# Attention and mixture of experts on one core: rank zero's token list made on its own, its row scales moved, two ranks narrower

## The chip, the cores and the metric

One NeuronCore of a Trainium2 chip runs the whole program. The metric is the device time of one execution in microseconds; of the runs made, the median counts. The names of the engines are those of the profile: PE is TensorE, DVE is VectorE, ACT is ScalarE, POOL is GpSimd, SP is SyncE, which only issues DMAs here.

## The reference

The attention comes first: 8 x 8 heads of 576 positions with 64 numbers each, a coarse attention over means of four positions and a local one over 7 neighbours, added up. Its output is the input x of a mixture of experts: 4608 tokens with 512 numbers, four groups of four experts. A token goes to the best expert of its best group.

```python
x = np.ascontiguousarray(attn_out.transpose(0, 2, 1, 3)).reshape(B * S, H * D)
g_idx = np.argmax(x @ w_group, axis=1)
...
e_idx = np.argmax(xg @ w_expert[g], axis=1)
...
h = np.maximum(xg[mask_e] @ w1[g, e], 0.0)
ye = h @ w2[g, e]
out[tok_idx] = combined[:, None] * ye      # combined: product of the two softmax weights
```

## The kernel before

The program runs in one pass over an order written out by hand (`ORDER`), then over a second list of steps (`begin`), then over the ranks (`main`). Each engine does its instructions in the order of these lists, and a wait of one of them holds all that stands behind it on that engine.

While the attention of the last batch still runs, the expert that has most of the first three quarters' tokens, up to 256, is done as the "early" one: 256 of its rows first, and what the last quarter adds as up to 128 "late" rows. `hidden f` is one block of 128 of its 1024 hidden numbers (12 products: four parts of 128 numbers, each matrix split in a high and a low part), `project f` carries a block into the output. The other 15 experts are put in order by their number of tokens ("ranks"). `ranks` makes that order on DVE (lines 813 to 820), `rank_lists` the token lists of all ranks (`choose`, lines 788 to 792, and `targets`, lines 797 to 799): `gi` holds the rows to fetch, `oi` the rows to store to.

`begin` first lets POOL fetch rank zero's rows (`gather`, `fetch`, line 925: an indirect DMA of 128 rows into `xg`, four of them, the last one for 32 rows) and SP load the first two of four quarters of its weights (`weights_in`, line 886). Then come the steps. The late rows run in four rounds: `hidden_rows` (12 products of 256 columns, line 1003, then the copy `hr` on ACT, line 1006), `turn_hidden` (two transposes, line 1011, then the copy `hrh` on ACT and the difference `hrl` on DVE, lines 965 and 966) and `project` (three products of 512 columns, line 1036). Between them stand the steps for rank zero: `scale` (ACT, line 939) multiplies the 512 numbers of the fetched rows by the token's weight, `turn_in k` (line 972) transposes the k-th 128 of them on PE, and ACT and DVE split them into `xh` and `xl` (lines 965 and 966). `weights_split` makes the high part of a quarter of the weights on ACT (line 894) and the low part on DVE (line 898). The low part frees the buffer for SP's next load. `arms` works out on DVE, in one number (`word`), which ranks need their full width; `choice` loads that number into the engines (line 1159).

In `main`, rank r multiplies its weights by CAPS[r] columns if it has more than CAPS[r] - LESS[r] tokens, and by CAPS[r] - LESS[r] columns otherwise (an If with two arms, for the ranks in SWITCHED). A rank has 96 hidden products (line 987) and 96 projecting ones (line 1038). The first hidden product of rank zero, behind the last projection of the late rows, begins `main`.

Of the kernel before, what the change touches and what calls it, by code (L numbers as in the profile page):

```python
# [34 lines left out]
NE = 16  # L35
# [7 lines left out]

QSCALE = SCALE / 16.0
CAPS = [416, 384, 368, 352, 336, 320, 312, 304, 296, 288, 280, 272, 264, 248, 240, 384]
LESS = [16 if r == 1 else 20 for r in range(16)]
SWITCHED = (0, 1, *range(3, 13))
TURNED = range(13)
SCATTER = (1, 3, 5, 8)
# [655 lines left out]
class Experts:  # L705
# [47 lines left out]
    def numbers(self):  # L753
# [7 lines left out]
        for j in range(NE):  # L761
            nc.gpsimd.memset(self.digit[:, j : j + 1], float(2**j))
            nc.gpsimd.memset(self.less[:, j : j + 1], -float(LESS[j]))

# [44 lines left out]
    def ranks(self):  # L809
# [9 lines left out]
        V.tensor_reduce(out=self.er, in_=self.big, axis=AX.X, op=ALU.add)  # L819
        V.tensor_copy(self.eri, self.er[0:1])  # L820

    def rank_lists(self):
        self.choose(0, NE - 1, self.roh[:, 0 : NE - 1], self.gi[:, 0 : NE - 1])
        self.targets(0, NE, self.oi)

    def fours(self):
# [277 lines left out]
    def begin(self, early, late, st):  # L1104

        V = self.nc.vector
        for n in ("w1", "w2"):
            for c in range(4):
                late[n, c] = early[n, c]
        self.gather(st)  # L1110
        e = self.expert(st)
        self.weights_in(st, e, 0)
        self.weights_in(st, e, 1)
        gathered = range(len(st["xg"]))
        steps = [
            (self.store, early, 0),
            (self.store, early, 1),
            (self.hidden_rows, late, 0),
            (self.weights_high, st, 0, "w1"),
            (self.hidden_rows, late, 1),  # L1120
            (self.turn_hidden, late, 0),
            (self.arms,),
            (self.hidden_rows, late, 2),
            (self.turn_hidden, late, 1),
            (self.weights_low, st, 0, "w1", V),
            (self.project, late, 0),
            (self.project, late, 1),
            *((self.scale, st, t) for t in gathered[:2]),
            (self.hidden_rows, late, 3),
            (self.turn_hidden, late, 2),  # L1130
            *((self.scale, st, t) for t in gathered[2:]),
            (self.project, late, 2),
            (self.project, late, 3),
            (self.choice,),
            (self.project, late, 4),
            (self.weights_split, st, 0, "w2", V),
            (self.weights_in, st, e, 2),
            (self.turn_in, st, 0),
            (self.turn_in, st, 1),
            (self.turn_hidden, late, 3),  # L1140
            (self.weights_split, st, 1, "w1", V),
            (self.project, late, 5),
            (self.turn_in, st, 2),
            (self.turn_in, st, 3),
            (self.fours,),
            (self.weights_split, st, 1, "w2", V),
            (self.weights_in, st, e, 3),
            (self.project, late, 6),
            (self.project, late, 7),
            (self.store, late, 0),  # L1150
        ]
        for f, *args in steps:
            f(*args)
        self.ys = [self.results(i, [P, 4 * P]) for i in range(4)]
        for y in self.ys:
            V.memset(y[:, CAPS[0] - LESS[0] : CAPS[0]], 0.0)

# [10 lines left out]
    def main(self, late, sts):  # L1168
        none = {"C": P, "xg": [], "y": []}
        sts = sts + [None]  # L1170
        with self.tc.manual_schedule():
            for r in range(NE - 2):
                pv = sts[r - 1] if r else none
                if r in SWITCHED:
# [3 lines left out]
                    with arm.Else():  # L1178
                        here[0] = dict(here[0], arm=CAPS[r] - LESS[r])
                        self.ranked(pv, *here, self.hint(r + 1))  # L1180
# [321 lines left out]
logits 15; scores_out 3; hidden 1; scores_turn 3; project 0; scores_turn_out 3; choose 3; choose_exp 3; choose_first 3; weight 3; hidden 2  # L1502
project 1; places 3; places_out 3; project 2; weights_split 2 w1 P; lists_places 3; lists 3 P; count 3; weights_split 2 w2 P; hidden 3
hidden 4; hidden 5; lists_add 3; early_list 0; gather_late; weights_split 3 w1 D; project 3; weights_split 3 w2 D; project 4; ranks
project 5; hidden 6; turn_late 0; turn_late 1; hidden 7; turn_late 2; turn_late 3; rank_lists; project 6; project 7
"""

@with_exitstack
# [111 lines left out]
```

## Time and profile before

| | us |
|---|---|
| median of 3 runs | 673.28 |
| lowest and highest | 669.38, 678.78 |
| the profiled execution | 675.54 |
| its span, first to last instruction | 673.8 |

The rows in this document are of the profiled execution. Times in a row count from the start of its span; 1.7 us of the profiled time lie outside the span. The mean granted TensorE clock was 0.988 of full speed.

### The profile page before, as it was taken

The page shows a single profiled execution, that of the slowest core. Times are in us where ns is not written, and L with a number is a line of the kernel's source. Part 1 is how long each engine was busy: PE and PEld are TensorE (multiplying, and loading weights), DVE is VectorE, ACT ScalarE, POOL GpSimd, SP SyncE. Part 2 cuts the span into 40 slices and gives each one's busy share as a digit, 9 for nine tenths or more (in the row PEclk, how much of TensorE's full clock was granted, in tenths as well). Part 3 has the DMA queues.
Part 4 walks back from the last instruction along what each step waited for, and adds up shares of the span by engine and source line. Part 5 has one row for each costly group of instructions (what it writes and reads, how often), then busy time and mean ns, then how long its engine had stood idle before and what let it go on. Part 6 is the DMA issues. An engine that isn't in the chain of part 4 may idle for free. (4 is left out here: it accounts for less than half of the span.)

```text
span 673.8 us, 17810 instructions
## 1 busy us (share of the span) xinstructions
PE 638.9 (95%) x6751; PEld 574.8 (85%) x6751; DVE 475.8 (71%) x968; ACT 382.5 (57%) x831; POOL 362.8 (54%) x418
## 2 busy tenths in 40 slices
PE   7898898998988898999999999999999999999996
PEld 3675676676766687999999999999999999999985
DVE  5886788778897586746666576766776786878751
ACT  7886665766764535644535345454464565556531
POOL 7974556576642554404463746657557556654521
PEclk7999999998998999999999999999999999999999
DMA  8799799979877816868686878879889879998920
GB/s 313 205 280 286 229 276 295 281 209 256 265 219 222 253 31 232 287 216 217 222 233 203 237 228 251 243 228 286 254 261 292 256 250 266 287 306 282 286 72 29
DMA packets 125903, 160.75 MB, mean 239 GB/s; under 512 B 23133, under 2 KB 90601, under 8 KB 125792
## 3 DMA queue, kind: packets, MB, share of 16 engines
q1 hardware_dynamic: 100032, 130.01, 63.8%
q0 software_dynamic: 8240, 20.47, 10.0%
q10 hardware_dynamic: 17520, 8.85, 4.9%
q8 instruction: 62, 1.02, 0.7%
q14 instruction: 49, 0.40, 0.2%
HBM read 129.51 MB, written 30.98 MB: 238 GB/s over the span
## 5 line engine op out<-in xcount | busy, mean ns | idle before, releaser
L1063 POOL DMA_INDIRECT out_dram<-yt,qo x135 | 153.6, 1137 | 138.5 <-DVE qo L838 109.5
L991 ACT ACTIVATE hh<-ph 128x368 fp32r<-128x368 f32 (+14 forms) x128 | 52.7, 413 | 185.7 <-PE ph L987 149.6
L987 PE MATMUL ph<-xh,w1h 128*128 128x368 f32 (+14 forms) x512 | 152.6, 299 | 0.0
L987 PE MATMUL ph<-xh,w1l 128*128 128x368 f32 (+14 forms) x512 | 152.4, 298 | 0.2 <-issue 0.2
L987 PE MATMUL ph<-xl,w1h 128*128 128x368 f32 (+14 forms) x512 | 152.4, 298 | 0.1
L1038 PE MATMUL y<-hh,w2h 128*128 128x368 f32 (+11 forms) x416 | 126.2, 303 | 0.0
L1038 PE MATMUL y<-hl,w2h 128*128 128x368 f32 (+11 forms) x416 | 125.7, 302 | 0.0
L1038 PE MATMUL y<-hh,w2l 128*128 128x368 f32 (+11 forms) x416 | 125.6, 302 | 0.0
L992 DVE SCALAR_TENSOR_TENSOR hl<-ph,hh 128x368 fp32r<-128x368 f32 (+14 forms) x128 | 58.5, 460 | 85.1 <-ACT hh L991 49.8
L987 PEld LDWEIGHTS ph<-xl,w1h 128*128 128x128 f32 x512 | 96.4, 188 | 0.8
L987 PEld LDWEIGHTS ph<-xh,w1h 128*128 128x128 f32 x512 | 96.2, 188 | 1.0 <-issue 0.2
L987 PEld LDWEIGHTS ph<-xh,w1l 128*128 128x128 f32 x512 | 96.4, 188 | 0.7 <-issue 0.6
L898 DVE TENSOR_TENSOR w2l<-raww,w2h 128x1024 fp32r<-128x1024 f32 x61 | 74.7, 1225 | 22.0 <-ACT w2h L894 14.8
L898 DVE TENSOR_TENSOR w1l<-raww,w1h 128x1024 fp32r<-128x1024 f32 x61 | 74.4, 1220 | 20.5 <-ACT w1h L894 10.7
L925 POOL DMA_INDIRECT xg<-xd,gi x47 | 55.4, 1179 | 53.9 <-ACT xh L965 23.9
L1038 PEld LDWEIGHTS y<-hl,w2h 128*128 128x128 f32 x416 | 78.3, 188 | 0.1
L1038 PEld LDWEIGHTS y<-hh,w2l 128*128 128x128 f32 x416 | 78.3, 188 | 0.0
L1038 PEld LDWEIGHTS y<-hh,w2h 128*128 128x128 f32 x416 | 78.2, 188 | 0.0
L894 ACT ACTIVATE w1h<-raww 128x1024 fp32r<-128x1024 f32 x64 | 67.4, 1054 | 2.6 <-DMA raww<-in_moe_w_dram 2.1
L894 ACT ACTIVATE w2h<-raww 128x1024 fp32r<-128x1024 f32 x64 | 67.1, 1051 | 0.8 <-DMA raww<-in_w2q_dram 0.7
L460 PE MATMUL b_x<-vw,pt 126*32 126x128 f32 x1152 | 39.0, 279 | 3.6 <-DMA vw<-odd 2.2
L460 PEld LDWEIGHTS b_x<-vw,pt 126*32 126x32 f32 x1152 | 31.0, 111 | 9.0 <-issue 6.9
(243 smaller groups left out, 1183.1 us busy)
## 6 DMA issues: line engine op xcount, KB each, us to landing
raww<-in_w2q_dram SPq DMA_DIRECT2D x52, 512.0 KB
raww<-in_w1q_dram SPq DMA_DIRECT2D x52, 512.0 KB
raww<-in_moe_w_dram SPq DMA_DIRECT2D x24, 512.0 KB
vw<-in_vw_dram SPq DMA_DIRECT2D x32, 378.0 KB
kt<-in_k_dram SPq DMA_DIRECT2D x16, 576.0 KB
qT<-in_q_dram SPq DMA_DIRECT2D x16, 576.0 KB
xd<-x ACTq DMA_DIRECT2D x15, 576.0 KB
vs<-in_vm_dram SPq DMA_DIRECT2D x16, 512.0 KB
```

Source lines behind the costliest of these rows:

```text
L460: self.nc.tensor.matmul(pt[32 * j : 32 * j + 32, t], self.of("pt", u)[:ROWS, 32 * lin : 32 * lin + 32], self.windows(u)[:ROWS, :, lin], st ...
L894: self.nc.scalar.activation(hi, self.raw[c % 2][n], AF.Copy)
L898: eng.tensor_tensor(out=lo, in0=self.raw[c % 2][n], in1=hi.bitcast(F32), op=ALU.subtract)
L925: self.nc.gpsimd.indirect_dma_start(out=xg[:w], out_offset=None, in_=self.xd[0:rows], in_offset=bass.IndirectOffsetOnAxis(ap=st["gi"][:w, ...
L987: nc.tensor.matmul(ph, a[:, k, cs], st[b][:, k, 0:C], start=(n == 0), stop=(n == 11))
L991: nc.scalar.activation(hh, ph, AF.Relu)
L992: nc.vector.scalar_tensor_tensor(out=hl, in0=ph, scalar=0.0, in1=hh.bitcast(F32), op0=ALU.max, op1=ALU.subtract)
L1038: nc.tensor.matmul(y, a[:, f % 2, cs], b, start=(f == 0 and n == 0), stop=(f == 7 and n == 2))
L1063: i = self.nc.gpsimd.indirect_dma_start(out=out, out_offset=bass.IndirectOffsetOnAxis(ap=index, axis=0), in_=y, in_offset=None, bounds_che ...
```

## The change

Three things change. `ORDER` gets a step `first_list` right behind `ranks`: it makes the list `gi` of rank zero alone; `rank_lists` makes the fourteen others, and the transposes of the late tile move behind `hidden 7`. In `begin`, the scales of rank zero's first three tiles stand between the late rows' earlier rounds; the split of the first quarter of w2 and the load of the third quarter stand ahead of the late rows' `project 3`; `project 4` moves behind `turn_hidden 3` and the split of the second quarter of w1. LESS is 28 and 24 for ranks three and four instead of 20.

```diff
-LESS = [16 if r == 1 else 20 for r in range(16)]
+LESS = [20, 16, 20, 28, 24] + 11 * [20]
...
+    def first_list(self):
+        self.choose(0, 1, self.roh[:, 0:1], self.gi[:, 0:1])
+
     def rank_lists(self):
-        self.choose(0, NE - 1, self.roh[:, 0 : NE - 1], self.gi[:, 0 : NE - 1])
+        self.choose(1, NE - 1, self.roh[:, 1 : NE - 1], self.gi[:, 1 : NE - 1])
         self.targets(0, NE, self.oi)
...
             (self.arms,),
+            (self.scale, st, 0),
             (self.hidden_rows, late, 2),
             (self.turn_hidden, late, 1),
             (self.weights_low, st, 0, "w1", V),
+            (self.scale, st, 1),
+            (self.scale, st, 2),
             (self.project, late, 0),
             (self.project, late, 1),
-            *((self.scale, st, t) for t in gathered[:2]),
             (self.hidden_rows, late, 3),
             (self.turn_hidden, late, 2),
-            *((self.scale, st, t) for t in gathered[2:]),
+            *((self.scale, st, t) for t in range(3, len(st["xg"]))),
             (self.project, late, 2),
+            (self.weights_split, st, 0, "w2", V),
+            (self.weights_in, st, e, 2),
             (self.project, late, 3),
             (self.choice,),
-            (self.project, late, 4),
-            (self.weights_split, st, 0, "w2", V),
-            (self.weights_in, st, e, 2),
             (self.turn_in, st, 0),
             (self.turn_in, st, 1),
             (self.turn_hidden, late, 3),
             (self.weights_split, st, 1, "w1", V),
+            (self.project, late, 4),
             (self.project, late, 5),
...
-project 5; hidden 6; turn_late 0; turn_late 1; hidden 7; turn_late 2; turn_late 3; rank_lists; project 6; project 7
+first_list; project 5; hidden 6; hidden 7; turn_late 0; turn_late 1; project 6; turn_late 2; turn_late 3; rank_lists; project 7
```

## Rows read from the trace of the kernel before

**Rows 1.** The page, busy time of each engine and its share of the span.

```profile
PE 638.9 (95%) x6751; PEld 574.8 (85%) x6751; DVE 475.8 (71%) x968; ACT 382.5 (57%) x831; POOL 362.8 (54%) x418
```

**Rows 2.** Waits of PE, 240 to 673 us: total us, times, longest.

```profile
PE y L1036 <- ACT hrh L965: 0.9, 1, 0.9
PE xt L972 <- DMA xg<-xd,gi: 0.7, 1, 0.7
PE xt L972 <- ACT xg L939: 0.6, 1, 0.6
PE xt L972 <- DVE xl L966: 0.5, 1, 0.5
...
```

**Rows 3.** Timeline of PE: start, us, operation, count, idle before it and its releaser.

```profile
249.29 0.44 PE L972 MATMUL xt<-idf,xg 128*128 128x128 f32 x2 [0.72 <-DMA xg<-xd,gi]
...
261.49 0.38 PE L1011 MATMUL ht<-idf,hr 128*128 128x128 f32 x2
...
264.14 0.50 PE L1036 MATMUL y<-w2h,hrh 128*128 128x512 f32 x1 [0.86 <-ACT hrh L965]
...
266.25 0.90 PE L972 MATMUL xt<-idf,xg 32*128 32x32 f32 x5 [0.59 <-ACT xg L939]
...
271.32 0.34 PE L987 MATMUL ph<-xh,w1h 128*128 128x396 f32 x1
```

**Rows 4.** Timeline of POOL: the fetches of the late tile and of rank zero.

```profile
245.09 1.77 POOL L925 DMA_INDIRECT xg<-xd,gi  x1 [0.81 <-DVE gi L792]
256.44 1.00 POOL L925 DMA_INDIRECT xg<-xd,gi  x1 [9.57 <-PE phr L1003]
...
260.35 2.07 POOL L925 DMA_INDIRECT xg<-xd,gi  x1 [0.30 <-DVE flag L1282]
```

**Rows 5.** Timeline of DVE: lists, ranks, and the differences of the late rows.

```profile
243.53 0.83 DVE L788 TENSOR_TENSOR sel<-tv,early 128x64 f32<-128x64 f32 x1
...
244.66 0.17 DVE L792 TENSOR_SCALAR gi<-rv 128x4 int32<-128x4 f32 x1
...
249.71 0.16 DVE L820 CAST eri<-er 1x16 int32<-1x16 f32 x1
...
252.39 1.88 DVE L788 TENSOR_TENSOR sel<-tv,roh 128x960 f32<-128x960 f32 x1
...
255.50 0.20 DVE L792 TENSOR_SCALAR gi<-rv 128x60 int32<-128x60 f32 x1
...
260.08 0.40 DVE L966 TENSOR_TENSOR hrl<-ht,hrh 128x256 fp32r<-128x256 f32 x1
260.41 1.20 DVE L898 TENSOR_TENSOR w1l<-raww,w1h 128x1024 fp32r<-128x1024 f32 x1
...
270.99 1.08 DVE L966 TENSOR_TENSOR xl<-xt,xh 128x416 fp32r<-128x416 f32 x2
```

**Rows 6.** Timeline of ACT: a weight copy, scales, and the third round's hr.

```profile
255.94 1.05 ACT L894 ACTIVATE w1h<-raww 128x1024 fp32r<-128x1024 f32 x1
...
262.14 1.40 ACT L939 ACTIVATE xg<-xg 128x512 f32<-128x512 f32 x2 [2.82 <-DMA xg<-xd,gi]
263.45 0.36 ACT L1006 ACTIVATE hr<-phr 128x256 f32<-128x256 f32 x1
...
265.47 0.72 ACT L939 ACTIVATE xg<-xg 32x512 f32<-32x512 f32 x1 [0.78 <-DMA xg<-xd,gi]
```

**Rows 7.** Busy time by stretch (PE, PEld, DVE, ACT, POOL), granted clock, DMA share, GB/s.

```profile
250.00:260.00 10.00, 10.00 (x70) 9.24 (x69) 7.84 (x22) 4.25 (x12) 2.95 (x3) 1.00 0.76 243
```

**Rows 8.** Line 1159, the choice's load in TensorE's sequencer: duration in ns, start.

```profile
L1159 PEldq TENSOR_LOAD <-word x1: 487/487/487, 260.5 to 260.5; - x1
```

**Rows 9.** Timeline of PE: the first products of ranks three, four and five.

```profile
372.90 0.32 PE L987 MATMUL ph<-xh,w1h 128*128 128x332 f32 x1
...
402.05 0.31 PE L987 MATMUL ph<-xh,w1h 128*128 128x316 f32 x1
...
429.89 0.30 PE L987 MATMUL ph<-xh,w1h 128*128 128x300 f32 x1
```

More of the change, by code (lines that the diff above doesn't have):

```diff
@@ L1113, in begin @@
         self.weights_in(st, e, 1)
-        gathered = range(len(st["xg"]))
         steps = [
```

## The prediction

> **What bounds the kernel now.** I read the page's busy line first: TensorE is busy 95% of the span [rows 1]. The chain of waits says nothing here: it holds only GpSimd's last store. So I asked who TensorE waited for, from 240 us to the end [rows 2]. The reader is to see that every wait of size lies before rank zero starts: 0.9 us for a copy of ScalarE, 0.7 us for a fetch, 0.6 us for a scaled tile, 0.5 us for VectorE. Behind 271.32 us, where the first product of rank zero starts, TensorE never waits for another engine again. Two things follow: what the stretch from 247 to 271 us loses is lost to the end, and a column taken from a later rank shortens the end by that column.
>
> The stretch itself I read engine by engine [rows 3 to 6]. Rank zero's list is written together with the fourteen others and is ready at 255.70 (255.50 + 0.20) [rows 5]. GpSimd's first fetch starts 0.74 us later, at 256.44 (the row names a product of TensorE, which only ended last; the fetch reads the list), and the four starts are 1.30 us apart, to 260.35 [rows 4]. ScalarE then idles 2.82 us for the first tile (262.14) and 0.78 us for the last (265.47) [rows 6], and since it works in order, the late rows' copies wait behind the scales: hr of round three comes at 263.45 though its products ended near 261.5 [rows 3, 6]. TensorE pays at 264.14 (0.86), 266.25 (0.59) and a little after [rows 2, 3].
>
> **The lists.** Three VectorE instructions go in right behind the cast of the ranks, which ends at 249.87 [rows 5]. Their cost has two bounds. The early expert's list took 1.30 us (243.53 to 244.83, 0.83 of it for the first), but there GpSimd was busy with a product of its own. Undisturbed, the list product of 960 elements takes 1.88, so 64 elements are 0.13 and a fixed part; three short instructions like the third (0.17) and the cast (0.16) make 0.65 with their starts. I take 0.65, because GpSimd is idle from 246.86 to 256.44 [rows 4]. The list is then ready at 250.5 and the first fetch starts 0.74 later, at 251.3; at 1.30 apart the others start at 252.6, 253.9 and 255.2. That the other fourteen lists are written later into the same tile shouldn't hold the fetch: at 271.32 rank zero's products read the first quarter of xl while VectorE writes the last ones until 272.07 [rows 3, 5], so a reader waits for its part of a tile alone.
>
> Who waits for the 0.65: hl of the early expert's sixth block stands behind it on VectorE, ready at 250.85 instead of 250.2. In the new order the seventh block's products (12 x 256 columns x 0.42 ns = 1.3 us, the price of a column is worked out below) stand ahead of the late tile's transposes, so TensorE no longer waits 0.72 for that tile [rows 3]: it landed by 249.3. But project six now comes sooner and waits about 0.5 for hl. Together that is 0.25 saved, or 0.4 lost at the 1.30 bound. The long list work starts some 0.7 later on VectorE and hands everything behind it (the second early store, the first hrl, the arms) on up to 0.7 later. Its cover is that hrl of round one, which ended at 260.48 [rows 5], is needed by project two only behind 261.49 [rows 3]; without that 1.0 us it would cost up to 0.7.
>
> **When the tiles land.** The first fetch was usable 5.7 us after its start (256.44 to 262.14), the fourth 5.1 (260.35 to 265.47) [rows 4, 6], with the DMA engines busy with weights. From the new starts that is 257.0 for the first and 260.3 for the last, 5.2 us earlier. ScalarE reaches scale zero at 257.7 (the weight copy ends at 256.99 [rows 6], two copies of about 0.38 follow), so it waits for nothing, and nothing of hr two, queued behind it, is held up. Scales one and two lie before round three's copy, in time that ScalarE idled away. What is late next is ScalarE's own order: round three's products end with the transposes at 261.49 [rows 3], 0.25 earlier now; then come hr three (from about 261.5, 0.36), hrh two (0.38) and the last scale (0.72), which ends near 262.9 instead of 266.19.
>
> From the end of the last scale to rank zero's first product it took 5.13 us (266.19 to 271.32): the second weight split, the transposes, projects five to seven. The split is moved ahead of project three in the program, but on ScalarE it still stands right behind the last scale and ahead of the first xh, and on VectorE ahead of the first xl, so this chain keeps its length. Project four is now inside it (three products of 512 columns, 0.65) and fills the 0.5 that TensorE waited there for VectorE [rows 2]: 5.13 + 0.2 to 5.4. Rank zero then starts at 262.9 + 5.4 = 268.3, **3.0 us earlier**. Cross-check: the four named waits are 2.7 us; the restart of the stream behind each adds some 0.2 to 0.3, and 0.5 of new waiting goes off: 2.2 to 3.4.
>
> **Other queues.** The choice's load of the arm word was taken by TensorE's sequencer at 260.5, over two microseconds ahead of its place in the stream [rows 8], and stays behind project three: nothing, or at most its 0.49 us if the sequencer is no longer ahead. On SyncE the third weight load is still released by w1l (260.41 + 1.20 [rows 5]); the fourth comes about 3 us earlier with the second split, and SyncE's own loads of the choice now queue behind it, to about 265. Only SyncE's next branch needs them, behind 268. GpSimd's fetches pass nothing. The first weight load now shares the DMA engines with the first fetch: 128 rows of 2112 bytes at the 243 GB/s of 250 to 260 us [rows 7] delay it by 1.1 us at the most; ScalarE would wait that long at 255.9 and has the later idle time to take it back: 0 to 0.5.
>
> **The narrower ranks.** A rank is 192 products (96 hidden, 96 projected). From 332 to 316 columns it shrinks from 29.15 us (372.90 to 402.05) to 27.84 us (402.05 to 429.89) [rows 9]: 1.31 / 16 = 0.082 us a column, 0.42 ns for each product. Eight columns are 0.66, four 0.33: **0.98 us**, all on the path. It holds only while both lists fit: over 324 rows rank three would run at 352, over 312 rank four at 336. Counted from the reference's own inputs and rules, these lists have 312 and 305 rows, so the narrow arms stay.
>
> **Sum.** 3.0 + 0.98 = 4.0 us off the profiled execution: 675.54 becomes 671.5. That run lay 2.26 above the median of the three, 673.28, which becomes **669.3**.
>
> **Rivals.**
> The tiles land later than I say. For it speaks that the four fetches now run beside 2 MB of weights, released by the same cast of the ranks at about 251, instead of behind half of them. If all these weights went first, they would be through at about 259.5 (2.1 MB at 243 GB/s from 251), and the 0.88 MB of 416 rows at 263.1: the last scale ends at 263.8, rank zero starts at 269.2, and the whole gains 3.1: 670.2. In addition the product of the fourteen lists lies over the fetches. The fetch at 260.35 took 2.07 us instead of 1.00 while w1l (two tiles read, 1.20 us) ran [rows 4, 5]; in that proportion the long product costs the fetches 1.07 x 1.75 / 1.20 = 1.6: in the same case 671.8. I take 671.0 for this rival. The Trainium skill (SBUF — State Buffer, "Who interferes with whom") speaks for this addition: a VectorE instruction with two SBUF inputs and a GpSimd one that reads SBUF exclude each other, and the second waits for the first to finish. The row agrees in direction, with 1.07 lost of the 1.20 that a full block could cost; by the rule alone the later fetches would lose up to 1.75 and the case end at 672.0.
>
> The change doesn't do what it says: the fetch is still released by the long list. Then it starts at 256.9, lands at 262.6, and as scale zero now stands ahead of hr two, hrh one, two scales, hr three, hrh two and the last scale (4.3 us in all with itself), rank zero starts at 262.6 + 4.3 + 5.4 = 272.3: 1.0 lost, 0.98 gained, 673.3.
>
> Slower: the same queue on ScalarE, with a late first tile. Each microsecond that tile zero lands behind 262.6 us moves the end by one. That is 11.3 us after its new start, twice the 5.7 of the trace. At 264.6 it costs 2 us: 675.3. Nothing in the rows shows a fetch that slow, but all copies of the late rows hang on it.
>
> **Chances.** Forecast 0.65, late tiles 0.18, no effect of the list 0.07, slower 0.05; 0.05 for what I don't see. The cases lie between 668.7 (3.6 us from the start) and 675.3. The three runs before spread from 669.38 to 678.78, and a median of three shares about half of that, so the range is 664.5 to 674.5. A measurement of this kernel can tell some 2% (13 us) from no change, and no case reaches that: faster 0.03, same 0.94, slower 0.03.
>
> **What would show it.** Right: the first fetch of rank zero near 251.3; no wait of ScalarE for a fetched tile; TensorE's wait for the late tile gone and one of about 0.5 for hl before project six; rank zero's first product near 268.3; ranks three and four at 28.5 and 27.5 us. Wrong: ScalarE idling before scale zero or one; fetches of 2 us; the first weight copy waiting for its load; a wait in rank zero or one for weights, which would give the gain back; a 352 in the widths.

## The result, and the profile after

The changed kernel takes 668.19 us (median of 20 runs, 664.78 to 673.80); the kernel before takes 677.42 in the runs beside it (20, 669.33 to 679.42). The ratio over the runs is 0.9896, with a 95% interval of 0.9869 to 0.9923 (the two medians alone would give 0.9864): about 1% faster, by the 2% bound the same. The forecast was 669.3 in 664.5 to 674.5. That sum was made against the median of the first three runs, 673.28; over all 20 the kernel before is 4 us higher, and where the extra difference comes from is asked below.

The profiled execution of the changed kernel took 667.74 us, with a span of 666.0, at a mean granted clock of 0.991 of full speed. The page's busy line, as [rows 1]:

```profile
PE 635.1 (95%) x6750; PEld 572.4 (86%) x6751; DVE 479.2 (72%) x971; ACT 384.6 (58%) x831; POOL 366.1 (55%) x418
```

TensorE is still the bound, and 3.8 us less busy. Its waits from 240 us on, as [rows 2] (us in total, times, longest), are now only these two:

```profile
PE y L1039 <- DVE hl L995: 0.5, 1, 0.5
PE xt L975 <- ACT xg L942: 0.4, 1, 0.4
```

The first is the wait for hl that was forecast ahead of project six. The second was not forecast. On VectorE's timeline (start, us, operation, idle before), as [rows 5], the short list stands behind the cast and the long one behind the late tile:

```profile
246.15 0.16 DVE L820 CAST eri<-er 1x16 int32<-1x16 f32 x1
246.24 0.25 DVE L788 TENSOR_TENSOR sel<-tv,roh 128x64 f32<-128x64 f32 x1
246.52 0.22 DVE L791 TENSOR_REDUCE rv<-sel 128x4 f32<-128x64 f32 x1
246.77 0.17 DVE L792 TENSOR_SCALAR gi<-rv 128x4 int32<-128x4 f32 x1
...
249.62 1.76 DVE L788 TENSOR_TENSOR sel<-tv,roh 128x896 f32<-128x896 f32 x1
```

Rank zero's fetches on GpSimd, as [rows 4]:

```profile
247.69 1.00 POOL L928 DMA_INDIRECT xg<-xd,gi  x1 [4.38 <-issue]
249.00 1.00 POOL L928 DMA_INDIRECT xg<-xd,gi  x1 [0.30 <-issue]
250.30 1.90 POOL L928 DMA_INDIRECT xg<-xd,gi  x1 [0.30 <-issue]
252.50 0.93 POOL L928 DMA_INDIRECT xg<-xd,gi  x1 [0.30 <-issue]
```

The list costs 0.70 us (246.24 to 246.94) and the first fetch starts 0.75 behind it. The third fetch is drawn out to 1.90 while VectorE forms the long list's product. ScalarE, as [rows 6]:

```profile
253.79 0.73 ACT L942 ACTIVATE xg<-xg 128x512 f32<-128x512 f32 x1
...
255.71 0.72 ACT L942 ACTIVATE xg<-xg 128x512 f32<-128x512 f32 x1 [0.16 <-DMA xg<-xd,gi]
258.33 0.73 ACT L942 ACTIVATE xg<-xg 128x512 f32<-128x512 f32 x1 [1.90 <-DMA xg<-xd,gi]
258.96 0.36 ACT L1009 ACTIVATE hr<-phr 128x256 f32<-128x256 f32 x1
259.22 0.37 ACT L968 ACTIVATE hrh<-ht 128x256 fp32r<-128x256 f32 x1
259.49 0.70 ACT L942 ACTIVATE xg<-xg 32x512 f32<-32x512 f32 x1
```

The first scale waits for nothing, the third waits 1.90 us for its tile, and hr of round three stands behind it: its products ended where the next transposes start, at 257.72. The DMA engines were full just then. Busy time by stretch (PE, PEld, DVE, ACT, POOL), granted clock, DMA share, GB/s:

```profile
247.00:250.00 3.00, 2.68 (x13) 2.17 (x14) 1.77 (x7) 1.04 (x6) 2.00 (x2) 1.00 0.43 142
250.00:253.00 3.00, 3.00 (x26) 2.96 (x25) 2.90 (x5) 1.53 (x3) 2.40 (x2) 1.00 1.04 378
253.00:256.00 3.00, 3.00 (x23) 2.82 (x23) 2.79 (x11) 2.44 (x7) 2.39 (x3) 1.00 1.09 398
```

That is only a little fuller than before the change. The share of 0.76 in [rows 7] is a mean over 10 us with a quiet start; in stretches of 3 us, some 3 to 10 us behind the cast as here, the kernel before has:

```profile
253.00:256.00 3.00, 3.00 (x22) 2.78 (x22) 2.90 (x5) 1.03 (x3) 0.00 (x0) 1.00 0.97 314
256.00:259.00 3.00, 3.00 (x27) 2.96 (x26) 2.15 (x6) 1.99 (x6) 2.00 (x2) 1.00 0.98 330
```

On TensorE's timeline, as [rows 3, 9], stand the first product of the early expert, the last transposes that rank zero waits for, and the first products of ranks zero, three, four and five:

```profile
223.44 0.38 PE L990 MATMUL ph<-xh,w1h 128*128 128x256 f32 x1
...
260.25 0.89 PE L975 MATMUL xt<-idf,xg 32*128 32x32 f32 x5 [0.42 <-ACT xg L942]
...
265.49 0.34 PE L990 MATMUL ph<-xh,w1h 128*128 128x396 f32 x1
...
367.06 0.31 PE L990 MATMUL ph<-xh,w1h 128*128 128x324 f32 x1
...
395.55 0.30 PE L990 MATMUL ph<-xh,w1h 128*128 128x312 f32 x1
...
423.09 0.30 PE L990 MATMUL ph<-xh,w1h 128*128 128x300 f32 x1
```

**Where the 7.8 us of the two spans lie.** The spans are 673.8 and 666.0. Before the change the early expert's first product came at 227.03:

```profile
227.03 0.36 PE L987 MATMUL ph<-xh,w1h 128*128 128x256 f32 x1
```

So 3.6 us had gone before any changed instruction ran (223.44 against 227.03; the attention's program is the same in both). From that product to the cast of the ranks both take 22.7. From the cast to rank zero it is 19.34 us (246.15 to 265.49) instead of 21.61 [rows 3, 5]: **2.3 us**. From rank zero to rank three both take 101.6. Rank three takes 28.49 instead of 29.15 and rank four 27.54 instead of 27.84 [rows 9]: **0.97 us**. One later rank, of 260 columns in both, took 24.16 us before and takes 23.03 now. Before, some of its products start late with no recorded cause; the one idle time that the trace names is 0.23 us, so most of the 1.1 us stays open:

```profile
565.04 0.37 PE L987 MATMUL ph<-xh,w1l 128*128 128x260 f32 x1 [0.23 <-issue]
```

That is 3.6 + 2.3 + 1.0 + 1.1 = 8.0, and the tail gives 0.1 back. What the change touches makes 3.3 of it.

### The profile page after: what moved, and what is told of

Same layout as the page of the kernel before. It is cut to its first block, busy times and chain, and to the rows that moved or that the text cites. A ratio compares the mean times of both kernels' runs of the same rounds, so it can differ in the third digit from the quotient of the medians.

```text
span 666.0 us, 17813 instructions
## 1 busy us (share of the span) xinstructions
PE 635.1 (95%) x6750; PEld 572.4 (86%) x6751; DVE 479.2 (72%) x971; ACT 384.6 (58%) x831; POOL 366.1 (55%) x418
## 3 DMA queue, kind: packets, MB, share of 16 engines
q0 software_dynamic: 8240, 20.47, 10.4%
## 5 line engine op out<-in xcount | busy, mean ns | idle before, releaser
L1066 POOL DMA_INDIRECT out_dram<-yt,qo x135 | 156.6, 1160 | 132.0 <-DVE qo L841 100.0
L969 DVE TENSOR_TENSOR xl<-xt,xh 128x256 fp32r<-128x256 f32 (+16 forms) x68 | 30.2, 449 | 13.8 <-ACT xh L968 13.7
```

What stands on the lines that cost most here:

```text
L969: self.nc.vector.tensor_tensor(out=lo, in0=x, in1=hi.bitcast(F32), op=ALU.subtract)
L1066: i = self.nc.gpsimd.indirect_dma_start(out=out, out_offset=bass.IndirectOffsetOnAxis(ap=index, axis=0), in_=y, in_offset=None, bounds_che ...
```

## The experiments

The main reading: the list is worth nearly the whole earlier start, the widths are worth their columns, and the moved scales are worth nothing or less, since the third tile isn't there yet. The rivals: list and scales are both needed; the long list's product beside the fetches costs the missing part; or the gain is a matter of the execution, not of the change. All stretches come from one profile of each kernel. The runs were made on several chips, so the times of different kernels are set only against the kernel before on the same chip, or not at all. The start is from the cast of the ranks to rank zero's first product.

| kernel | start, us | rank three, us | rank four, us | span, us |
|---|---|---|---|---|
| before | 21.61 | 29.15 | 27.84 | 673.8 |
| the change | 19.34 | 28.49 | 27.54 | 666.0 |
| before, again | 21.69 | 29.15 | 27.85 | 671.1 |
| the change, again | 19.12 | 28.49 | 27.54 | 672.0 |
| widths alone | 21.69 | 28.49 | 27.54 | 670.3 |
| list and scales, old widths | 19.48 | 29.14 | 27.85 | 670.4 |
| list alone | 18.88 | 29.15 | 27.85 | 668.0 |
| moved steps alone | 21.97 | 29.15 | 27.85 | 672.2 |
| third scale later | 18.99 | 28.49 | 27.54 | 669.7 |
| long list late | 21.11, again 18.85 | 28.49 | 27.54 | 672.9, 667.7 |
| list and widths | 18.84 | 28.49 | 27.54 | 666.2 |
| list and widths, long list late | 18.84 | 28.49 | 27.54 | 664.3 |
| list behind hl, and widths | 22.26 | 28.49 | 27.55 | 671.6 |

**The kernel before, run as if it were a change.** No edit.

> The kernel before once more, unchanged, timed against itself. Theory (the change gains only in the stretch between the ranks and rank zero's first product, 2.3 us by the traces, and in ranks three and four, 1.0 us; what the 20 runs show beyond these 3.3 us is scatter of the attention): ratio within 0.5% of 1, and its own profile may show the first product of the early expert anywhere between 223 and 228 us. Rival (the changed program is faster in the attention too, by 3 to 4 us): ratio 1 as well, but the first product of the early expert stays near 227 us.

Measured: 673.31 us, ratio 0.9965 (0.9925 to 1.0005). So 0.35% can appear without a change, and a difference of that size says nothing. The first product of the early expert comes at 224.58 us here and at 227.03 in the first profile of the same program: its place scatters by itself.

**The changed kernel, once more**, on the chip of the run above. No edit.

> The changed kernel once more. Theory: cast of the ranks to rank zero's first product 19.3 us again instead of 21.6, ranks three and four 28.49 and 27.54 us, ratio 0.995 on the average, scattering by half a per cent with the attention. Rival: ratio 0.990 again, and the first product of the early expert again near 223 us.

Measured: 671.70 us, ratio 0.9917 (0.9882 to 0.9951). Against the kernel before run beside it as a change that is 0.9917 / 0.9965 = 0.9952, some 3.2 us; the two medians are 1.6 us apart. The first ratio, 0.9896, is not contradicted, but the part that goes beyond 0.5% is of the size that no change shows too. The trace again has the two terms, 2.5 at the start and 0.97 in the ranks. The early expert's first product comes at 222.30, as the rival had it. But in the fourteen profiles it lies at 222.65 to 227.03 with the list of before (four kernels) and at 222.30 to 226.22 with the early list (ten), so no gain ahead of it is shown. And yet the profiled span is 672.0, 6.0 us longer than the other profile of the same program. TensorE's waits from 421 to 672 us, where the first profile has none, are:

```profile
PE y L1041 <- issue: 1.6, 4, 0.4
PE ph L990 <- issue: 1.6, 3, 0.9
```

They make 3.2 of the 7.4 us that this profile is longer from rank five to the end.

**The widths alone.**

```diff
-LESS = [16 if r == 1 else 20 for r in range(16)]
+LESS = [20, 16, 20, 28, 24] + 11 * [20]
```

> The kernel before with the narrower ranks three and four alone. Theory: rank three 28.49 us and rank four 27.54 us, 0.97 us in all, nothing else: ratio 0.9985, cast of the ranks to rank zero's first product 21.6 us. Rival: a changed program shifts the attention too, so that the ratio is below 0.995 although only 1.0 us of products are gone.

Measured: 673.14 us, ratio 0.9968 (0.9934 to 1.0001), which is what no change gave beside it; the time tells nothing. The trace does: ranks three and four are shorter by 0.66 and 0.31, and the start is that of before, 21.69.

**List and scales with the old widths** (the line above undone in the changed kernel).

> The changed kernel with the old widths. Theory: cast of the ranks to rank zero's first product 19.3 us, ranks three and four 29.15 and 27.85 us, ratio 0.9965. Rival: ratio 0.991 or below, with the rest of the gain ahead of the early expert's first product.

Measured: 674.55 us, ratio 0.9965 (0.9933 to 0.9996); again too small for the time alone. The start is 19.48: all of its gain is there without the widths, so the two parts add.

**The list alone**, with the steps and widths of before. The order is the changed one, so the late tile's transposes move too.

```diff
+    def first_list(self):
+        self.choose(0, 1, self.roh[:, 0:1], self.gi[:, 0:1])
...
-        self.choose(0, NE - 1, self.roh[:, 0 : NE - 1], self.gi[:, 0 : NE - 1])
+        self.choose(1, NE - 1, self.roh[:, 1 : NE - 1], self.gi[:, 1 : NE - 1])
...
-project 5; hidden 6; turn_late 0; turn_late 1; hidden 7; turn_late 2; turn_late 3; rank_lists; project 6; project 7
+first_list; project 5; hidden 6; hidden 7; turn_late 0; turn_late 1; project 6; turn_late 2; turn_late 3; rank_lists; project 7
```

> Rank zero's list alone and the late tile's transposes as in the changed kernel, but the steps of the start (scales, project four, weight split) and the widths as before. Theory (the gain of the start is the earlier fetch; where the scales stand hardly matters, since the tiles land before ScalarE needs them or set the pace in either order): cast of the ranks to rank zero's first product 19.2 to 19.6 us, as in the changed kernel. Rival (the moved scales and project four carry a good part): 20.3 us or more.

Measured: 669.78 us in a single run, start 18.88: 2.7 us earlier than before, 0.2 to 0.6 earlier than with the moved scales, and better than either reading had expected. The cast and rank zero's first product:

```profile
245.99 0.16 DVE L820 CAST eri<-er 1x16 int32<-1x16 f32 x1
264.87 0.34 PE L990 MATMUL ph<-xh,w1h 128*128 128x396 f32 x1
```

No run takes the list and the moved transposes apart. But the transposes lie ahead of the late rows' first product, and that comes 4.1 us behind the cast (250.10) instead of 4.3 (254.00 before the change): they can hold some 0.2 of the 2.7. ScalarE's timeline:

```profile
255.50 1.52 ACT L942 ACTIVATE xg<-xg 128x512 f32<-128x512 f32 x2
257.85 0.39 ACT L1009 ACTIVATE hr<-phr 128x256 f32<-128x256 f32 x1 [0.83 <-PE phr L1006]
258.13 0.38 ACT L968 ACTIVATE hrh<-ht 128x256 fp32r<-128x256 f32 x1
258.43 1.34 ACT L942 ACTIVATE xg<-xg 128x512 f32<-128x512 f32 x2
```

No scale waits as much as 0.2 us for its tile here, and hr three waits for TensorE, as it should: with the old steps the third tile is asked for behind that copy, at 258.43, 12.4 us behind the cast, and has landed by then.

**The moved steps alone** (the `begin` part of the diff, with lists, order and widths of before).

> The steps of the start as in the changed kernel, the lists in one piece and the widths as before: scale zero stands ahead of hr two, but the tile lands as late as before. Theory (ScalarE's order turns the late tile into a wait of all late copies): ScalarE idles some 4 us before scale zero, and cast of the ranks to rank zero's first product is 22.0 to 22.6 us, longer than the 21.6 of before. Rival (the late rounds have slack enough, or the fetch was never bound by the long list): 21.6 or less.

Measured: 673.91 us in a single run, start 21.97: not earlier than before, rather 0.3 later. ScalarE, with the scale now ahead of hr two, waits for a fetch that starts as late as it did:

```profile
256.66 0.72 ACT L939 ACTIVATE xg<-xg 128x512 f32<-128x512 f32 x1 [3.40 <-DMA xg<-xd,gi]
```

TensorE waits 1.8 us in one piece for a scaled tile, and 0.48 ahead of that with no recorded cause:

```profile
257.71 0.44 PE L1011 MATMUL ht<-idf,hr 128*128 128x128 f32 x2 [0.48 <-issue]
...
262.07 0.90 PE L972 MATMUL xt<-idf,xg 32*128 32x32 f32 x5 [1.81 <-ACT xg L939]
```

Without that 0.48 the start could be as low as 21.5 (an estimate), so a loss of 0.3 is not shown. The steps are no gain of their own; they only don't hurt much once the list is early.

**The third scale behind round three's copies**, in the changed kernel.

```diff
             (self.scale, st, 1),
-            (self.scale, st, 2),
...
-            *((self.scale, st, t) for t in range(3, len(st["xg"]))),
+            *((self.scale, st, t) for t in range(2, len(st["xg"]))),
```

> The changed kernel with the third tile's scale behind the third turn_hidden, together with the last. Theory (in the changed kernel the third tile lands late, ScalarE waits 1.9 us for it, and hr three is held up): no wait of ScalarE before hr three, which comes some 1.0 us sooner, but the last two scales then still wait for the same tile: cast to rank zero's first product 0.1 to 0.3 us shorter than in the changed kernel, 18.9 to 19.2. Rival (hr three was on the path): 0.8 us shorter or more.

Measured: 671.51 us in a single run, start 18.99. Nothing of ScalarE waits for the third tile any more (hr three waits 1.38 for its own products), and 0.1 to 0.5 of the start comes back.

**The long list at the end of the steps**, in the changed kernel.

```diff
             (self.turn_in, st, 3),
+            (self.rank_lists,),
...
-first_list; project 5; hidden 6; hidden 7; turn_late 0; turn_late 1; project 6; turn_late 2; turn_late 3; rank_lists; project 7
+first_list; project 5; hidden 6; hidden 7; turn_late 0; turn_late 1; project 6; turn_late 2; turn_late 3; project 7
```

> The changed kernel with the fourteen other lists made behind the last transposes of rank zero, far from the four fetches. Theory (VectorE's product of the long list held up the third fetch, 1.9 us instead of 1.0, and made its tile late): all four fetches take 1.0 us, ScalarE waits less than 1.0 us for the third tile, and cast to rank zero's first product is 0.4 to 0.8 us shorter, 18.4 to 18.9; the rank lists then come late for rank zero's own work, which may lose more than that behind it. Rival (the tile is late because of the weights on the DMA engines): the third fetch takes 1.0 us, but its tile lands no sooner, and the stretch stays at 19.1 to 19.4.

Measured: 674.62 us in a single run, start 21.11, later by 1.8 than with the change. The fetches are all of 0.93 to 1.00 us. But ScalarE waits for TensorE, and TensorE for nothing recorded (ScalarE's copy, then TensorE's transposes):

```profile
255.32 0.39 ACT L1009 ACTIVATE hr<-phr 128x256 f32<-128x256 f32 x1 [2.41 <-PE phr L1006]
```

```profile
255.75 0.44 PE L1014 MATMUL ht<-idf,hr 128*128 128x128 f32 x2 [1.21 <-issue]
```

One run couldn't tell an accident of the execution from a new order that hurts. So the same kernel ran once more:

> The changed kernel with the fourteen lists behind the transposes, a second look, the same kernel as in the first. There ScalarE idled 2.4 us before the second round's hr, whose products had ended, and the stretch took 21.1 us. Theory A (ScalarE ran out of instructions at this place of its program, which the moved list doesn't touch): the idle time is there again or not, by chance; without it the stretch takes 18.4 to 19.0 us. Theory B (the moved list causes it): 2.4 us again and 21.1.

Measured: 669.46 us in a single run, start 18.85. The gap is gone, so the late list alone does not make it; what does is open. Its third fetch and its third scale:

```profile
252.49 1.00 POOL L928 DMA_INDIRECT xg<-xd,gi  x1 [0.30 <-issue]
```

```profile
259.12 0.73 ACT L942 ACTIVATE xg<-xg 128x512 f32<-128x512 f32 x1 [0.79 <-DMA xg<-xd,gi]
```

With the product of the long list out of the way the third scale starts 10.8 us behind the cast (248.33) instead of 12.2, and hr three no longer stands behind it. So that product costs the change some 0.3 to 0.6 us (18.85 against 19.12 to 19.48).

**List and widths, the old steps.**

> Rank zero's list alone, the late tile's transposes and the narrower ranks as in the changed kernel, the steps of the start as before. Theory (the list earns the whole gain, the moved scales lose some 0.3 to 0.6 us of it): cast of the ranks to rank zero's first product 18.8 to 19.0 us, ranks three and four 28.49 and 27.54, together 3.7 us less than the kernel before and 0.4 less than the changed one; by the clock of the whole kernel, where the unchanged one came out at 0.9965 of itself, 0.987 to 0.996. Rival (the look at the list alone was a lucky one): 19.2 to 19.5 us.

Measured: 667.86 us, ratio 0.9890 (0.9854 to 0.9925), start 18.84. Its interval covers the change's two ratios: by the trace it gains 0.3 to 0.6 us on the change, by the time nothing that can be told.

**The same with the long list at the end.**

> As the kernel with the list and the widths, with the fourteen lists behind the last transposes. Theory (in that kernel TensorE is the bound of the stretch, the tiles are not): the third fetch takes 1.0 us instead of 1.9, its tile lands 1 us sooner, and the stretch stays at 18.8 to 19.0 us. Rival (the tiles are still on the path): 18.5 or less. If ScalarE idles 2 us or more before the second hr, as in the other kernel with the late list, the cause is the late list and the stretch takes 20 us or more.

Measured: 666.00 us in a single run, start 18.84, the same as with the product beside the fetches. The second scale still waits 0.35 us for its tile, but no copy that TensorE needs stands behind it, and so a freer fetch gives nothing: what is left is TensorE's own work, with 0.5 of waiting for hl.

**The short list behind hl of block six**, with the old steps and the new widths, to take that 0.5 too.

```diff
-first_list; project 5; hidden 6; hidden 7; turn_late 0; turn_late 1; project 6; turn_late 2; turn_late 3; rank_lists; project 7
+project 5; hidden 6; first_list; hidden 7; turn_late 0; turn_late 1; project 6; turn_late 2; turn_late 3; rank_lists; project 7
```

> As the kernel with the list and the widths, but rank zero's list made behind hl of the sixth block instead of ahead of it. Theory (what is left in this stretch is TensorE's wait of 0.5 us for that hl; the fetches come 0.4 us later, which TensorE's stream has room for): the wait ahead of project six is gone, the first fetch starts 1.9 us behind the cast instead of 1.5, and the stretch takes 18.4 to 18.75 us. Rival (the tiles set the pace, and the later fetch hands its 0.4 us on): 18.9 us or more.

Measured: 669.63 us, ratio 0.9914 (0.9878 to 0.9949), start 22.26 in the profile. The wait for hl is gone, but the first fetch starts 1.87 us behind the cast (248.91) instead of 1.54, and the second one lies under the long list's product:

```profile
250.78 1.00 POOL L928 DMA_INDIRECT xg<-xd,gi  x1 [4.71 <-issue]
252.08 2.26 POOL L928 DMA_INDIRECT xg<-xd,gi  x1 [0.30 <-issue]
```

```profile
258.30 0.73 ACT L942 ACTIVATE xg<-xg 128x512 f32<-128x512 f32 x1 [0.65 <-DMA xg<-xd,gi]
262.44 0.72 ACT L942 ACTIVATE xg<-xg 128x512 f32<-128x512 f32 x1 [3.41 <-DMA xg<-xd,gi]
```

The second tile comes 10.4 us after its fetch began, where the change's second took 6.7. TensorE loses 2.2 to a copy behind it, and after that wait its granted clock falls: it is 1.00 up to 265 us, 0.57 from 265 to 269 (the mean of 4 us, and nearly all at the lower level, 1.2 GHz, up to 267), and 1.00 again behind it. The product that waited, the eight transposes that follow, and the stretch (columns as above):

```profile
263.76 0.50 PE L1039 MATMUL y<-w2h,hrh 128*128 128x512 f32 x1 [2.16 <-ACT hrh L968]
...
264.79 1.91 PE L975 MATMUL xt<-idf,xg 128*128 128x128 f32 x8
```

```profile
265.00:269.00 4.00, 4.00 (x17) 2.69 (x15) 2.77 (x5) 3.11 (x5) 0.00 (x0) 0.57 0.16 47
```

With the list alone these eight transposes take 1.32 us (from 259.91). By the profile 3.4 us are lost against list and widths: 1.7 of waiting (2.16 less the 0.5 for hl that is gone) and, as an estimate, 1.7 of clock (4.0 x 0.43). The timed ratio is only 0.0024 above that of list and widths, inside the intervals. So the profile shows a bad case, and how often it comes is open.

## Why the prediction was right, and where it wasn't

The size came out near, 668.19 against 669.3, but partly by luck: the terms forecast 4.0 us, the traces give the change 3.3, and the two timed comparisons 7.0 and 5.6 us (0.0104 and 0.0083 of 677). Taken off the later median, 677.42, the same terms would have given 673.4. In the profiles the rest lies where nothing was changed: over the fourteen profiles the early expert's first product comes anywhere from 222.3 to 227.0 us, and the stretch from rank five to the end differs by over 7 us for equal instructions. What sets that is open.

**The list: right.** 0.70 us against 0.65, the first fetch 0.75 behind it against 0.74. The fetch does not wait for the other fourteen lists: the rival by which the list has no effect, 673.3, is out, and the list alone, with the transposes that move with it, gives 2.7.

**The landing of the tiles: too early, and this is the term that was mis-sized.** The prediction had ScalarE wait for nothing, with tiles 5.1 to 5.7 us after their fetches. The first took up to 6.1 (253.79 - 247.69; its scale didn't wait), the second 6.7, and the third 8.0, whose scale waited 1.90. Two causes stood in the rival of the late tiles. The long product is shown: it held up the third fetch by 0.90 us, and with the product out of the way the third scale starts 1.4 us sooner (10.8 us behind the cast instead of 12.2). The weights on the DMA engines are not: the engines were nearly as full over the same stretch before the change, and no run moved a load. But the early fetches begin 1.5 to 6.4 us behind the cast, early in that stretch, where the old ones began 6.7 to 10.6 behind it. And tiles whose fetch no product held up are late too: in six of the profiles with the early list a scale that waited for such a tile started 6.6 to 7.5 us after the fetch began, where the prediction had 5.1 to 5.7. That fits the rival and does not prove it. The forecast let round three's copy go ahead as soon as its products were done; in the change it started 12.8 us behind the cast (258.96), 1.0 later than the forecast's 11.8. With the long list out of the way it started at 11.8 (260.15 against 248.33), and the last scale ended 13.1 behind the cast where 13.2 was forecast and the change has 14.0. So the missed part of the start is this queue: the end of the last scale was forecast 0.8 us too early.

**The block of the fetch is not in proportion.** The prediction scaled it by the product's length, 1.07 x 1.75 / 1.20. The rows of ten profiles give another rule: the fetch of rank zero that is drawn out ends 0.81 to 0.83 us after VectorE's product, whenever it began: at 262.42 behind 261.61 before the change [rows 4, 5], at 252.20 behind 251.38 after it, at 254.34 behind 253.52 with the list behind hl. The loss is what is left of the product when the fetch begins, less 0.18. That agrees with the rule of the Trainium skill (SBUF — State Buffer, "Who interferes with whom") that the second of two such instructions waits for the first to finish. It is not the whole rule by the trace: the change's second fetch had run for 0.62 us when the product began (249.00 and 249.62); it kept its 1.00, and the product its 1.76, as without a fetch (1.75 to 1.79). The prediction took the 1.07 of 1.20 for a partial block; the rows fit a whole one that began a little late.

**From the last scale to rank zero: right in the change.** 5.30 us (260.19 to 265.49) against 5.4. But this isn't a chain of fixed length: with the last scale at 13.1 it is 5.8, and four kernels in three orders end at 18.84 to 18.88. In these TensorE waits for nothing in the stretch but the 0.5 for hl, so its own work is the limit, and the forecast's 3.0 was not to be had: 21.6 - 18.84 is 2.8.

**The wait for hl: right**, 0.5 us. Taking it away by moving the list was not worth it: it starts the fetches later.

**The scales: the wrong credit.** The prediction gave the moved scales a part in letting ScalarE go ahead. The list alone gains 2.7, the steps alone gain nothing, and both together gain 2.1 to 2.6. A scale that is put ahead of a copy that TensorE needs is only as early as its tile.

**The widths: right.** 0.66 + 0.31 = 0.97 against 0.98; the ranks run at 324 and 312 columns. **The choice's load: right.** It lies at 256.7 in TensorE's sequencer (0.75 us), and no wait follows it. **The slower rival**, a late tile that holds up the copies behind it, did not decide here but is real: its mechanism is what cost the list behind hl 3.4 us in its profile, half of it by the wait and half by the granted clock that fell after it. The prediction had no term for the clock.

## What to carry to other kernels

When a transfer that the bound engine waits for is released by a batch of work, make the part it needs first and by itself: three short instructions, with the late tile's transposes moved behind them, bought 2.7 us here, while reordering its consumers bought nothing. An in-order engine should not be given a step that waits for a transfer ahead of one that the bound engine waits for; place it by the latest landing that the traces show, since that moves with the order itself. And a wait of the bound engine can cost more than its length: 2.2 us of waiting took some 1.7 more in granted clock in one profile here. And when an edit is worth half a per cent, compare the stretches that it touches and run the kernel before against itself, since the total can move as much for other reasons.

## What the runs showed that was not expected

- A gather's issue on GpSimd that begins under a VectorE product of two operands, or 0.06 us ahead of it, ends 0.81 to 0.83 us behind that product (ten profiles, fetches of 1.90 to 2.26 us instead of 1.00). The late tile's fetch (245.09 to 246.86 in [rows 4]) shows much the same under a low part of the weights, `w1l` on VectorE, that ends at 245.96 (244.73 + 1.23), 0.90 ahead of it. A fetch that began 0.62 us ahead of the product was not held.
- TensorE stands still in some executions with no recorded cause: one profile of the changed kernel takes 7.4 us more from rank five to the end than the other (250.3 against 242.9) for the same instructions, 3.2 of it in recorded gaps. After one such gap the granted clock fell, from 535 to 540 us in the longer profile (columns as above):

```profile
530.00:535.00 5.00, 4.13 (x34) 4.10 (x33) 3.01 (x5) 1.88 (x3) 3.78 (x5) 1.00 1.11 257
535.00:540.00 5.00, 4.26 (x22) 3.90 (x22) 2.02 (x5) 3.49 (x6) 2.49 (x3) 0.72 0.97 308
```

  The DMA engines were full there; but they are also full in stretches without a gap (1.04 to 1.09 after the change, with TensorE busy throughout), so that alone doesn't make one.
- A scale that waited for its tile started 6.6 to 8.2 us after the fetch began in the profiles with the early list, and 10.4 after it in one, against 4.3 to 6.1 with the list of before. The hold-up of a fetch explains up to 1.3 of it; the rest is open.
- The granted clock of TensorE fell to 0.57 over 4 us behind a wait of 2.2 us, in the profile with the list behind hl; in the other thirteen it is 1.00 from the cast to rank zero.
